# Gated linear attention and a soft mixture of experts: blocks of 128 tokens in place of two chunks of 64, y made transposed, odd head pairs reversed in time, and a combination in four row tiles

## The chip, the cores and the metric

The kernel runs on one core of a Trainium2 chip. The metric is the device time of one execution in microseconds (us). The engines of the core are named as in the profile: PE (matrix multiply; PEld is its weight load), DVE (VectorE), ACT (ScalarE), POOL (GpSimd) and SP (the queue that issues all the DMAs). Each engine works through its own queue in order, and waits where an operand isn't ready yet.

## The reference

First comes a linear attention with a decay, for 4 batches x 8 heads, 768 tokens, head size D = 48:

```
f = 1 / (1 + exp(-f_logit))
for t in range(S):
    state = f[:, :, t, :, None] * state + einsum('bhd,bhe->bhde', k[:, :, t], v[:, :, t])
    y[:, :, t] = einsum('bhd,bhde->bhe', q[:, :, t], state)
```

Its output, as x of 3072 tokens x 384, goes through a soft mixture with 32 slots, four for each of 8 experts:

```
logits = x @ phi                                   # 3072 x 32
d = softmax of logits over the tokens              # per slot
slot_input = d.T @ x                               # 32 x 384
slot_out[e] = relu(slot_input[e] @ w1[e]) @ w2[e]  # 384 -> 1024 -> 384, per expert
c = softmax of logits over the slots               # per token
out = c @ slot_out                                 # 3072 x 384
```

Everything is float32.

## The kernel before

**Attention.** Six blocks of 128 tokens for each of 4 batches make 24 blocks. A tile holds the 8 heads as 4 head pairs: the first head of a pair in partitions 0 to 47, the second in 64 to 111. The recurrence is turned into matmuls by the running sum of ln(1 + exp(-f_logit)) inside a chunk of C = 64 tokens, two chunks in a block; the second head of each pair is stored with its two chunks exchanged. exp and ln (L374, L377) are made for two blocks at once on ACT. Then, for each block: the scan L395 (DVE, 512 elements wide; `chain` is 0 where a new sum begins), the exponentials g and p (L398, L401, ACT), the decay of whole chunks `pend` (L405, L406, two copies on POOL), k times g and q times p (L409, L412, POOL). PE transposes k (L417), and L420 copies it to SBUF. L441 makes k^T v of both chunks (16 small matmuls), and DVE adds that to the state and multiplies by the decay, once for each chunk (L444 and L449, 192 wide). L460 multiplies q by the states (16 matmuls of 48 columns), L430 makes the scores k^T q (16 matmuls of 64 columns), L433 masks the later keys out of them (DVE, 512 wide), and L470 adds scores times v to the result of L460 (16 matmuls of 48 columns). L476 copies y to SBUF with tokens in the partitions (`xr`); L509 transposes it (3 transposes) and L512 copies that to `xT`.

**Mixture in the block phase.** Every four blocks a *unit* makes the logits (L527) with their maximum and exponential over tokens (L533, L536), transposes both (L539, L542), multiplies the exponential by x (L546, L549), and takes the softmax over the slots of its 512 tokens (L555 to L578, tiles `ce` and `cm`). The last two steps, L575 and L578, split the result into a high and a low part in the fp32r format (tile `c`), which L583 transposes and L586 copies to `cts`.

**Tail.** Maximum over all units, L643 (slot inputs), L682 (the product with w1, 48 matmuls of 512 columns), relu, transposes, L716 (the product with w2, in three parts of 128 output columns), and for each part L741: six matmuls of 128 x 512 in fp32r, copied out by L747 and stored by L751, 128 output columns x 512 tokens each.

**What sets the order.** All operations are given to a planner (`Plan`), which lays out every engine's queue ahead of time: of the operations that are ready it takes the one that can start first, and among those within 0.12 us of each other the one with the lowest due time, `T(n, stage) = 3.6 * n + stage` for block n. Durations come from formulas such as `t_dve`. PSUM is planned the same way: three two-bank tiles ("pair") for L441, L460 with L470, and L430, and two one-bank tiles ("one", `sg` in the profile) for the rest. Twelve 8 KB homes (`hm`) take w1; w2 goes into buffers of the block phase that have come free.

The scan, for example, is a single line over the whole block, and its place in DVE's queue is the planner's choice:

```
add(f"scan{n}", {"DVE": 0.06 + 0.0021 * 512}, scan, r=[L, "chain"], w=[CB], prio=T(n, 1))
add(f"g{n}", {"ACT": t_act(512)}, exp_g, r=[CB], w=[G], prio=T(n, 1.4))
```

Of the kernel before, what the change touches and what calls it, by code (L numbers as in the profile page):

```python
# [9 lines left out]
F32R = mybir.dt.float32r  # L10
# [6 lines left out]
C = 64  # L17
BT = 128
NB = S // BT
NN = B * NB  # L20
# [15 lines left out]
NX = 8  # L36
# [28 lines left out]
def t_dve(n, psum=False):  # L65
    return 0.09 + 0.00105 * n + (0.06 if psum else 0)


def t_pool(n):
    return 0.1 + 0.0023 * n  # L70


def t_pe(n):

    return 0.06 + 0.00086 * n


class Plan:
# [40 lines left out]
    def schedule(self):  # L119
# [13 lines left out]
        while ready:  # L133
            best = None
            for n in ready:
                op = ops[n]
                for e, us in op["eng"].items():
# [5 lines left out]
                    if op["kind"]:  # L143
                        if not pool[op["kind"]]:
                            continue
                        t = max(t, min(pool[op["kind"]])[0] + self.LAT)
# [14 lines left out]
            if op["kind"]:  # L161
                x = min(pool[op["kind"]])
                pool[op["kind"]].remove(x)
                self.bank[op["psum"]] = (op["kind"], x[1])
# [29 lines left out]
def gla_soft_moe_kernel(ctx: ExitStack, tc: tile.TileContext, q, k, f, v, fd, kd, vd, phi, w1, w2, out):  # L194
# [17 lines left out]

    pairs = [pp.tile([128, 2, 512], F32, tag=f"pr{i}", name=f"pr{i}") for i in range(3)]
    ones_ = [pp.tile([128, 512], F32, tag=f"sg{i}", name=f"sg{i}") for i in range(2)]
    plan = Plan({"pair": [0, 1, 2], "one": [0, 1]})

    def bank(handle):
        kind, x = plan.bank[handle]
        return (pairs if kind == "pair" else ones_)[x]


    AF_, AK, AQ, AV, AC, AP = (P([128, HOME], n) for n in ("af", "ak", "aq", "av", "ac", "ap"))
    homes = [P([128, HOME], f"hm{i}") for i in range(NHOME)]
    NK, NQ, NV, NC, NSS = 4, 4, 4, 3, 4

    def part(t, x, n, **kw):
        return t[:, x : x + n].rearrange("p (a t) -> p a t", **kw)

    fb = [AF_[:, 1024 * i : 1024 * i + 1024].rearrange("p (n a t) -> p n a t", n=2, a=PR) for i in range(2)]
# [3 lines left out]
    cb = [part(AC, 512 * i, 512, a=PR) for i in range(NC)]  # L233
    gb = [part(AV, 1536, 512, a=PR), part(AC, 1536, 512, a=PR)]
    kp = [part(AP, 512 * i, 512, a=H) for i in range(2)]
    sc = [AP[:, 1024 + 512 * i : 1536 + 512 * i].rearrange("p (r a t) -> p r a t", r=2, a=PR) for i in range(2)]
    st = [P([128, PR, D], f"st{i}") for i in range(NSS)]
    sa = [P([128, PR, D], f"sa{i}") for i in range(2)]
    xr = P([128, NX, DM], "xr")
    xT = P([128, 3, UB, 128], "xT")  # L240
    cts = P([128, NN, 128], "cts", F32R)
    c4 = P([128, UB, 4, NS], "c4", F32R)
    ce, cm = P([128, UB, NS], "ce"), P([128, UB], "cm")
    el = P([128, 2, 128], "el")
    lt, et = P([128, 128], "lt"), P([128, 128], "et")
    pin = P([128, NU, DM], "pin")

    nmx, sms = P([128, NU], "nmx"), P([128, NU], "sms")
    ident, ones, same = (P([128, 128], n) for n in ("ident", "ones", "same"))
    tri, chain = P([128, C], "tri"), P([128, 2 * PR, C], "chain")  # L250
    phs = P([128, 3, NS], "phs")
    pend = P([128, NN, 2, PR], "pend")
# [4 lines left out]
    s4, sob = P([128, DM], "s4", F32R), P([128, DM], "sob")  # L257
    hx = P([128, 512], "hx")
    gok, gbad = P([128, 4], "gok"), P([1, 1], "gbad", I32)
    hs = [flat(xT)[:, 512 * i : 512 * i + 512] for i in range(3)] + [hx]  # L260
    hT = flat(xr)[:, :2048].rearrange("p (j k m) -> p j k m", j=2, k=8)
    ARENA = {
        "af": (AF_, [("f", i) for i in range(2)] + [("f", i, x) for i in range(2) for x in range(2)]),
        "ak": (AK, [("k", i) for i in range(NK)]),
        "ac": (AC, [("c", i) for i in range(NC)] + [("g", 1)]),
        "ap": (AP, [("kp", i) for i in range(2)] + [("sc", i) for i in range(2)]),
        "aq": (AQ, [("q", i) for i in range(NQ)]),
        "av": (AV, [("v", i) for i in range(NV)] + [("g", 0)]),
# [15 lines left out]
    def c_tri(e):  # L284

        for c in range(2):
            cs = slice(C * c, C * c + C)
            nc.gpsimd.affine_select(tri[cs], ones[cs, :C], pattern=[[1, C]], compare_op=ALU.is_ge, fill=0.0, base=0, channel_multiplier=-1)

    def c_chain(e):  # L290

        nc.vector.memset(chain, 1.0)
        nc.vector.memset(chain[:, :, 0], 0.0)
# [4 lines left out]
    def c_kv(e):  # L298
        for t in pairs:
            nc.vector.memset(t, 0.0)  # L300
# [19 lines left out]
    add("chain", {"DVE": 0.4}, c_chain, w=["chain"])  # L320
    add("ident", {"POOL": 0.8}, c_ident, w=["ident"])
    add("tri", {"POOL": 0.5}, c_tri, r=["ones"], w=["tri"], prio=1)
    add("kv0", {"DVE": 2.4}, c_kv, w=["kv0"])
    add("same", {"DVE": 0.5}, c_same, r=["ident"], w=["same"], prio=20)
    add("emask", {"POOL": 1.0}, c_emask, w=["emask"], prio=30)
    for x in range(9):
        add("warm", {"PE": 0.3}, warm(x), r=["ones"], w=["warm"], prio=100)


    homes_ = [(t, [("home", i)]) for i, t in enumerate(homes)]  # L330
# [3 lines left out]
    w2at, at = {}, 0  # L334
    for p, j, kh in W2:
        w2at[p, j, kh] = at
        at += 16 * (CUT[p + 1] - CUT[p])

    def load_w1(x):
        t = w1p[W1[x]]  # L340
        return lambda e: nc.sync.dma_start(t, w1[x])

    def load_w2(p, j, kh):
        n = 16 * (CUT[p + 1] - CUT[p])
        t, at = w2p[p, j, kh], w2at[p, j, kh]
        return lambda e: nc.sync.dma_start(t[:, :n], w2[:, at : at + n])


    def T(n, stage):
        return 3.6 * n + stage  # L350
# [7 lines left out]
    def load_f(n, cnt):  # L358
        i, o = n // 2 % 2, n % 2
        load(fb[i][:, o : o + cnt], f[:, n : n + cnt], f"f{n}", [("f", i, x) for x in range(o, o + cnt)], T(n, -10), 262144 * cnt)  # L360

    def loads(n):
        load(kb[n % NK], k[:, n], f"k{n}", [("k", n % NK)], T(n, -8.5), 262144)
        load(qb[n % NQ], q[:, n], f"q{n}", [("q", n % NQ)], T(n, -8), 262144)
        load(vb[n % NV], v[:, n], f"v{n}", [("v", n % NV)], T(n, -7), 196608)

    def exp_f(n, cnt):

        i, o = n // 2, n % 2
        es = n if n < 2 else i + 1  # L370
        t = flat(fb[i % 2][:, o : o + cnt])
        ks = [("f", i % 2, x) for x in range(o, o + cnt)]
        add(
            f"exp{n}", {"ACT": t_act(512 * cnt) + 0.09}, lambda e: nc.scalar.activation(t, t, AF.Exp, scale=-1.0, accum_out=esum[:, es : es + 1]),  # L374
            w=[*ks, "esum"], prio=T(n, 0),
        )
        add(f"ln{n}", {"ACT": t_act(512 * cnt)}, lambda e: nc.scalar.activation(t, t, AF.Ln, bias=1.0), w=ks, prio=T(n, 0.5))  # L377

    def block(n):
        b, m = divmod(n, NB)  # L380
        l_ = fb[n // 2 % 2][:, n % 2]
        c_, g_, k_, q_, v_, kp_, sc_ = cb[n % NC], gb[n % 2], kb[n % NK], qb[n % NQ], vb[n % NV], kp[n % 2], sc[n % 2]
        L, CB, G, K, Q, V, KP, SC = ("f", n // 2 % 2, n % 2), ("c", n % NC), ("g", n % 2), ("k", n % NK), ("q", n % NQ), ("v", n % NV), ("kp", n % 2), ("sc", n % 2)
        X = ("x", n % NX)
        x_ = xr[:, n % NX]

        S = [("st", (2 * n + j) % NSS) for j in range(3)]
        s_ = [st[(2 * n + j) % NSS] for j in range(3)]
        steps = [j for j in range(2) if (m, j) != (NB - 1, 1)]
        begun = [j for j in range(2) if (m, j) != (0, 0)]  # L390
# [3 lines left out]
        def scan(e):  # L394
            nc.vector.tensor_tensor_scan(flat(c_), flat(chain), flat(l_), 0.0, op0=ALU.mult, op1=ALU.add)  # L395

        def exp_g(e):
            nc.scalar.activation(flat(g_), flat(c_), AF.Exp)  # L398

        def exp_p(e):  # L400
# [572 lines left out]
```

## Time and profile before

| | before |
|---|---|
| median of 3 runs | 220.26 us (218.66 to 224.37) |
| the profiled execution | 220.23 us, of which the profile's span is 218.5 us |
| mean granted PE clock | 0.84 |
| PE busy | 163.8 us (75%) |
| DVE busy | 129.3 us (59%) |
| ACT busy | 103.1 us (47%) |
| POOL busy | 82.6 us (38%) |
| moved by DMA | 54.22 MB |

Busy time counts an engine's instructions; a matmul in float32 leaves two records. The span falls into a start (until the first transposes of k, at 9.95 us), the block phase (until the last y is in SBUF, at 156.26 us), and the tail. In a timeline the columns are start, duration, engine, line, operation, output <- inputs, number of instructions, and in brackets the engine's idle time before it with what ended it.

### The profile page before, as it was taken

How to read it: one execution, taken by the hardware profiler on the slowest of the kernel's cores; microseconds unless marked ns; L12 is line 12 of the kernel's file. 1: busy time of each engine (PE TensorE's matmuls, PEld its weight loads, DVE VectorE, ACT ScalarE, POOL GpSimd, SP SyncE). 2: the span in 40 equal slices, each digit the busy share in tenths (PEclk: the TensorE clock that was granted, in tenths of full speed). 3: DMA queues.
4: the chain of work that ended last, by engine and by line, in shares of the span. 5: the costliest groups of instructions: out<-in, count | busy, mean ns of one | idle time of the engine just before them, and what ended most of it. 6: DMA issues, size and time to landing. Idle time of an engine off the chain costs nothing.

```text
span 218.5 us, 9188 instructions
## 1 busy us (share of the span) xinstructions
PE 163.8 (75%) x4046; PEld 119.8 (55%) x4046; DVE 129.3 (59%) x257; ACT 103.1 (47%) x198; POOL 82.6 (38%) x116
## 2 busy tenths in 40 slices
PE   7487879839586786994498866888764999699840
PEld 7476767628464575764386655756523234565510
DVE  7677785797979592369669999987360023010120
ACT  4466655382654645528567774734330112025540
POOL 3145875470777404505994834980000000000000
PEclk9967665896999796559589999999955699999975
DMA  6999998688798498959546644545694499507491
GB/s 188 343 392 404 390 297 283 214 256 307 228 348 306 140 357 281 393 156 329 174 143 186 165 157 142 157 171 195 202 387 187 139 351 418 250 6 288 185 359 51
DMA packets 17874, 54.22 MB, mean 248 GB/s; under 512 B 2336, under 2 KB 5408, under 8 KB 14752
## 3 DMA queue, kind: packets, MB, share of 16 engines
q1 hardware_dynamic: 17824, 53.53, 69.5%
q8 instruction: 34, 0.56, 1.0%
q14 instruction: 16, 0.13, 0.2%
HBM read 48.81 MB, written 4.72 MB: 245 GB/s over the span
## 4 chain that ended last, share of the span: by engine, by line
PE 37%; DVE 16%; issue 13%; ACT 10%; POOL 5%; DVEq 0%; POOLq 0%; ACTq 0%
PE sg L682 6%; PE sg L716 5%; DVE st L449 4%; PE pr L460 3%; PE sg L417 3%; POOL ak L409 3%; DVE ac L395 3%; PE pr L470 3%; PE sg L741 3%; PE pr L430 3%; ACT hm L747 2%; PE sg L509 2%; DVE ap L433 2%; PE pr L441 2%; PE sg L527 2%
## 5 line engine op out<-in xcount | busy, mean ns | idle before, releaser
L412 POOL TENSOR_TENSOR aq<-aq,ac 128x512 f32<-128x512 f32 x23 | 31.4, 1364 | 2.5 <-issue 1.9
L395 DVE TENSOR_TENSOR_SCAN ac<-chain,af 128x512 f32<-128x512 f32 x24 | 30.3, 1268 | 1.7 <-POOL pend L406 1.5
L409 POOL TENSOR_TENSOR ak<-ak,av 128x512 f32<-128x512 f32 x11 | 15.2, 1383 | 40.0 <-issue 27.3
L470 PE MATMUL pr<-av,ap 64*64 64x48 f32 x768 | 19.4, 244 | 11.1 <-DVE ap L433 9.2
L417 PE MATMUL sg<-ident,ak 128*128 128x128 f32 x96 | 19.3, 338 | 8.4 <-POOL ak L409 5.7
L470 PEld LDWEIGHTS pr<-av,ap 64*64 64x64 f32 x768 | 16.2, 155 | 15.9 <-DVE ap L433 12.3
L449 DVE TENSOR_TENSOR st<-sa,pend 128x192 f32<-128x192 f32 x35 | 23.3, 665 | 2.1
L460 PE MATMUL pr<-st,aq 48*64 48x48 f32 x704 | 22.2, 247 | 2.8 <-DVE st L449 2.1
L430 PE MATMUL pr<-aq,ak 48*64 48x64 f32 x768 | 20.3, 243 | 4.1 <-issue 4.1
L460 PEld LDWEIGHTS pr<-st,aq 48*64 48x64 f32 x704 | 18.4, 158 | 7.3 <-DVE st L449 3.0
L430 PEld LDWEIGHTS pr<-aq,ak 48*64 48x64 f32 x768 | 17.1, 154 | 5.6 <-issue 5.6
L433 DVE TENSOR_TENSOR ap<-pr,tri 128x512 f32<-128x512 f32 x24 | 16.3, 680 | 5.6 <-PE pr L430 5.5
L417 PEld LDWEIGHTS sg<-ident,ak 128*128 128x128 f32 x96 | 13.1, 170 | 11.5 <-POOL ak L409 6.7
L409 POOL TENSOR_TENSOR ak<-ak,ac 128x512 f32<-128x512 f32 x11 | 15.0, 1368 | 10.2 <-issue 7.4
L420 ACT COPY ap<-sg 128x512 f32<-128x512 f32 x21 | 12.3, 584 | 13.5 <-PE sg L417 13.2
L441 PE MATMUL pr<-av,ap 64*48 64x48 f32 x704 | 15.8, 233 | 2.6 <-ACT ap L420 1.7
L444 DVE TENSOR_TENSOR sa<-pr,st 128x192 f32<-128x192 f32 x40 | 14.1, 352 | 6.1 <-ACT xr L476 1.9
L441 PEld LDWEIGHTS pr<-av,ap 64*48 64x48 f32 x704 | 13.2, 145 | 5.5 <-ACT ap L420 2.4
L509 PE MATMUL sg<-ident,xr 128*128 128x128 f32 x72 | 14.8, 322 | 1.3 <-ACT xr L476 1.3
L401 ACT ACTIVATE ac<-ac 128x512 f32<-128x512 f32 x24 | 15.2, 631 | 0.6
L374 ACT ACTIVATE af<-af 128x1024 f32<-128x1024 f32 (+1 forms) x13 | 12.9, 992 | 4.4 <-DMA af<-in_f_dram 4.4
L476 ACT COPY xr<-pr 128x384 f32<-128x384 f32 x17 | 8.1, 477 | 14.3 <-PE pr L470 14.2
(125 smaller groups left out, 257.6 us busy)
## 6 DMA issues: line engine op xcount, KB each, us to landing
hm<-in_w_dram SPq DMA_DIRECT2D x18, 1024.0 KB, 7.6
ak<-in_k_dram SPq DMA_DIRECT2D x24, 256.0 KB, 4.1
aq<-in_q_dram SPq DMA_DIRECT2D x24, 256.0 KB, 4.3
af<-in_f_dram SPq DMA_DIRECT2D x11, 512.0 KB, 6.0
av<-in_v_dram SPq DMA_DIRECT2D x24, 192.0 KB, 4.7
out_dram<-hm SPq DMA_DIRECT2D x6, 512.0 KB, 2.8
out_dram<-hm SPq DMA_DIRECT2D x6, 256.0 KB, 3.0
af<-in_w_dram SPq DMA_DIRECT2D x1, 1024.0 KB, 4.7
```

The source lines that it names most:

```text
L395: nc.vector.tensor_tensor_scan(flat(c_), flat(chain), flat(l_), 0.0, op0=ALU.mult, op1=ALU.add)
L401: nc.scalar.activation(flat(c_), flat(c_), AF.Exp, scale=-1.0)
L409: tt(e)(flat(k_), flat(k_), flat(g_), op=ALU.mult)
L412: tt(e)(flat(q_), flat(q_), flat(c_), op=ALU.mult)
L417: nc.tensor.transpose(pk[:, a], k_[:, a], ident)
L430: nc.tensor.matmul(ps[half[c], r, a], k_[rows[r], a, half[c]], q_[rows[r], a, half[c]], start=True, stop=True)
L433: tt(e)(sc_, sc_at(), tri.unsqueeze(1).unsqueeze(1).broadcast_to([128, 2, PR, C]), op=ALU.mult)
L441: nc.tensor.matmul(pk[C * r : C * r + D, j, a], kp_[half[c], h, :D], v_[half[c], h], start=True, stop=True)
L449: tt(e)(s_[j + 1], src, pend[:, n, j].unsqueeze(2).broadcast_to([128, PR, D]), op=ALU.mult)
L460: nc.tensor.matmul(py[half[j], r, a], q_[rows[r], a, half[j ^ r]], s_[j][rows[r], a], start=a == 0, stop=False, skip_group_check=True)
L470: nc.tensor.matmul(py[half[j], r, a], sc_[half[c], r, a], v_[half[c], 2 * a + r], start=j not in begun and a == 0, stop=a == PR - 1, skip_ ...
L509: nc.tensor.transpose(px[:, c], x_[:, 128 * c : 128 * c + 128], ident)
```

## The change

**Blocks of 128.** The chunk is now the block: one sum over 128 tokens, one state step for each block. Odd head pairs are stored reversed in time (k, q, f and v), and their scans L381 and L382 run apart: one forward over the two even pairs, one backward over the two odd ones. The exponentials (L396, L397) and the copies of `pend` are made for two blocks at once. L451 (k^T v) has 8 matmuls with 128 rows, into a one-bank tile; there is one L454 and one L458 for each block.

**y transposed.** L468 and L477 have the states and v as stationary operand, and q and the scores as moving one: 8 matmuls of 128 columns each. The result has head dimensions in the partitions, so L480 copies it straight to `xT`, and what is transposed (L510, 4 transposes) is the `xr` that L546 needs. The logits (L527) have 4 padded row groups instead of 3 (16 matmuls).

**No scores of later keys.** In L439 a key of the second half meets 64 queries only, a key of the first half 128; the scores have a two-bank tile of their own, and the mask L442 is 1024 wide for a block.

**Slot softmax.** It keeps the logits in `ltok`, is made for two units at once (256 wide), without a split in two parts, and its due time lies behind the block phase: `T(NN, 12)`.

**Combination.** For each of three parts there are four groups of two float32 matmuls of 32 rows x 384 columns, each in its own row tile; L735 copies 768 columns, and 384 KB are stored for each group.

**Loads.** q, k, v and f are contiguous for each block in DRAM; w1 and w2 come as four runs of 2 KB for each partition in place of one of 8 KB. Two more PSUM tiles are cleared at the start, and the warming matmuls wait for that. The planner has other duration formulas for DVE and POOL, and a pace of 3.8 in place of 3.6 in `T`.

```diff
-    plan = Plan({"pair": [0, 1, 2], "one": [0, 1]})
+    plan = Plan({"sc": [0], "pair": [1, 2], "one": [0, 1]})
...
     def T(n, stage):
-        return 3.6 * n + stage
+        return 3.8 * n + stage
...
+        def scan(x):
+            def fn(e):
+                cx, lx = flat(cb[i % 2][:, x]), flat(fb[i % 2][:, x])
+                nc.vector.tensor_tensor_scan(cx[:, : 2 * BT], chain, lx[:, : 2 * BT], 0.0, op0=ALU.mult, op1=ALU.add)
+                nc.vector.tensor_tensor_scan(cx[:, 2 * BT :][:, ::-1], chain, lx[:, 2 * BT :], 0.0, op0=ALU.mult, op1=ALU.add)
+            return fn
...
+        for x in xs:
+            add(f"scan{n + x - o}", {"DVE": 2 * t_scan(256)}, scan(x), r=[ks[x - o], "chain"], w=[cs[x - o]], prio=T(n + x - o, -1))
+        add(f"g{n}", {"ACT": t_act(w)}, lambda e: nc.scalar.activation(flat(g_), flat(c_), AF.Exp), r=cs, w=gs, prio=T(n, 1))
...
         def scores(e):
-            ps = sc_at()
+            ps = bank(("sc", n)).rearrange("p r (a t) -> p r a t", a=PR)
             for a in range(PR):
                 for c in range(2):
+                    at = half[c ^ (a % 2)]
                     for r in range(2):
-                        nc.tensor.matmul(ps[half[c], r, a], k_[rows[r], a, half[c]], q_[rows[r], a, half[c]], start=True, stop=True)
+                        nc.tensor.matmul(ps[at, r, a, HT * c :], k_[rows[r], col(a), at], queries(r, a)[:, HT * c :], start=True, stop=True)
...
         def kv(e):
-            pk = bank(("kv", n))[:, :, : PR * D].rearrange("p j (a e) -> p j a e", a=PR)
+            pk = bank(("kv", n))[:, : PR * D].rearrange("p (a e) -> p a e", a=PR)
             for a in range(PR):
-                for j in steps:
-                    for r in range(2):
-                        h, c = 2 * a + r, j ^ r
-                        nc.tensor.matmul(pk[C * r : C * r + D, j, a], kp_[half[c], h, :D], v_[half[c], h], start=True, stop=True)
...
+                for r in range(2):
+                    nc.tensor.matmul(pk[rows[r], col(a)], kp_[:, col(a), rows[r]], v_[:, 2 * a + r], start=True, stop=True)
...
         def inter(e):
             py = y_at()
             for a in range(PR):
-                for j in begun:
-                    for r in range(2):
-                        nc.tensor.matmul(py[half[j], r, a], q_[rows[r], a, half[j ^ r]], s_[j][rows[r], a], start=a == 0, stop=False, skip_group_check=True)
+                for r in range(2):
+                    at = 64 * (r ^ (a % 2))
+                    nc.tensor.matmul(py[at : at + D, r, a // 2], s0[rows[r], col(a)], queries(r, a), start=a < 2, stop=False, skip_group_check=True)
...
         def intra(e):
             py = y_at()
             for a in range(PR):
-                for c in range(2):
-                    for r in range(2):
...
+                for r in range(2):
+                    at = 64 * (r ^ (a % 2))
+                    nc.tensor.matmul(py[at : at + D, r, a // 2], v_[:, 2 * a + r], sc_[:, r, a], start=first and a < 2, stop=a >= 2, skip_group_check=True)
...
+    def slots(th):
+        x = slice(2 * UB * th, 2 * UB * th + 2 * UB)
...
+        sp = T(NN, 12) + th
...
         def combine(p, x):
...
+            def fn(e):
+                for y in range(2):
+                    gs = slice(64 * (x % 2) + 32 * y, 64 * (x % 2) + 32 * y + 32)
+                    nc.tensor.matmul(
+                        bank(("cb", p, x))[:, y, :384], s4[gs, CUT[p] : CUT[p + 1]], cts[gs, 3 * (x // 2) : 3 * (x // 2) + 3], start=True, stop=True,
+                    )
+            return fn
```

Two places show what the planner makes of this. On DVE, before, in the middle of the block phase: the slot softmax of unit 2 (L564 to L578), the two state steps of block 13, and then the scan of block 14:

```order
L564 TENSOR_REDUCE cm<-ce 128x4
L565 TENSOR_SCALAR cm<-cm 128x4
L566 RECIPROCAL cm<-cm 128x4
L569 TENSOR_TENSOR ce<-ce,cm 128x128
L575 CAST c_94<-ce 128x8x32
L476 COPY xr<-pr_62 128x2x4x48
L578 TENSOR_TENSOR c_94<-ce,c_94 128x8x32
L444 TENSOR_TENSOR sa_89<-pr_63,st_87 128x192
L449 TENSOR_TENSOR st_88<-sa_89,pend 128x192
L444 TENSOR_TENSOR sa_90<-pr_63,st_88 128x192
L449 TENSOR_TENSOR st_85<-sa_90,pend 128x192
L395 SCALAR_TENSOR_TENSOR ac<-chain,af 128x512
```

After, on DVE near the same scan: the state step and the mask of block 10, then both scans of block 14 (those of block 15 and the mask of block 11 follow):

```order
L454 TENSOR_TENSOR sa<-sg_66,st_89 128x192
L458 TENSOR_TENSOR st_90<-sa,pend 128x192
L442 TENSOR_TENSOR as<-pr_62,tri 128x1024
L381 SCALAR_TENSOR_TENSOR ac<-chain,af 128x256
L382 SCALAR_TENSOR_TENSOR ac<-chain,af 128x256
```

The scan of block 14 has moved from behind the mask of block 12 to a place ahead of the mask of block 11, and no slot softmax stands ahead of it there. The slot softmax of units 0 to 3 still stands on DVE among the masks of later blocks, that of units 4 and 5 behind the last one.

On PE, before, at blocks 6 to 9: scores of block 7, transposes of x of block 6, of k of block 8, L470 of block 7, L441 of block 8, and transposes of k of block 9 and of x of block 7:

```order
L430 MATMUL pr_62<-aq,ak 64x64 x16
L509 MATMUL sg_66<-ident,xr 128x128 x3
L417 MATMUL sg_65<-ident,ak 128x128 x4
L470 MATMUL pr_64<-av,ap 64x48 x16
L441 MATMUL pr_63<-av,ap 48x48 x16
L417 MATMUL sg_66<-ident,ak 128x128 x4
L509 MATMUL sg_65<-ident,xr 128x128 x3
```

After, on PE, at the same blocks: transposes of k of block 8 and of y of block 6, L477 of block 7, L451 of block 8, L468 of block 8 and the transposes of y of block 7:

```order
L428 MATMUL sg_65<-ident,ak 128x128 x4
L510 MATMUL sg_66<-ident,xT 128x128 x4
L477 MATMUL pr_63<-as,av 48x128 x8
L451 MATMUL sg_65<-av,kp_86 48x48 x8
L468 MATMUL pr_64<-aq,st_90 48x128 x8
L510 MATMUL sg_66<-ident,xT 128x128 x4
```

A block has fewer and wider matmuls, and L451 now takes its turn with the transposes in the two `sg` tiles. Along PE's queue in the block phase the shape of the tile (128 rows by 128 columns, 64 by 64, 128 by 64 and so on) changes 136 times, against 104 before.

503 lines of the change are left out of this document (232 added, 271 removed).

## The prediction

> **What bounds the kernel now.** I read the page first, then the busy time of each stage, then the timeline where engines wait.
>
> ```profile
> span 218.5 us, 9188 instructions
> PE 163.8 (75%) x4046; PEld 119.8 (55%) x4046; DVE 129.3 (59%) x257; ACT 103.1 (47%) x198; POOL 82.6 (38%) x116
> PEclk9967665896999796559589999999955699999975
> PE 37%; DVE 16%; issue 13%; ACT 10%; POOL 5%; DVEq 0%; POOLq 0%; ACTq 0%
> ```
>
> No engine is full. The chain that ended last is spread over PE, DVE and ACT, as where short steps hand over to each other; PE leads it. The clock row is uneven in the first half and flat at 9 in most of the second. The timeline gives the stages:
>
> ```profile
> 9.95 0.63 PE L417 MATMUL sg<-ident,ak 128*128 128x128 f32 x4 [2.51 <-issue]
> ...
> 155.78 0.48 ACT L476 COPY xr<-pr 128x384 f32<-128x384 f32 x1 [0.55 <-PE pr L470]
> ...
> 168.76 0.26 PE L643 MATMUL sg<-wd,pin 128*32 128x32 f32 x1 [3.24 <-issue]
> 169.47 5.21 PE L682 MATMUL sg<-hm,si 128*32 128x512 f32 x32
> ...
> 185.09 1.08 PE L716 MATMUL sg<-af,xr 128*32 128x128 f32 x32
> ...
> 210.99 0.58 ACT L747 COPY hm<-sg 128x512 f32<-128x512 f32 x1
> ```
>
> The start takes 9.95 us; the blocks run until 156.26 (155.78 + 0.48), 146.3 us or 6.10 for each of 24; then 13.2 us to the first product with w1, 15.6 to the first with w2, 26.5 until the last copy (211.57), and 6.9 for the last store. Two thirds of the time lie in the blocks, so the windows there decide, first over all engines, then for the masks L433 alone, which count the blocks:
>
> ```profile
> core 0: us, PE busy (x) PEld busy (x) DVE busy (x) ACT busy (x) POOL busy (x), PEclk, DMA share, GB/s
> 10.00:30.00 20.00, 15.62 (x438) 12.90 (x438) 15.46 (x26) 13.37 (x23) 13.01 (x16) 0.73 1.02 382
> 10.00:110.00 100.00, 75.69 (x2012) 60.32 (x2016) 71.78 (x130) 56.22 (x107) 54.33 (x65) 0.77 0.84 291
> 110.00:158.00 48.00, 38.23 (x1326) 30.30 (x1319) 39.93 (x82) 27.98 (x55) 25.96 (x34) 0.99 0.53 168
> 10.00:158.00 148.00, 113.92 (x3326) 90.62 (x3327) 111.71 (x212) 84.20 (x161) 80.29 (x98) 0.84 0.74 251
> ```
>
> ```profile
> 10.00:110.00 100.00, 9.53 (x14) 0.77 0.84 291
> 110.00:158.00 48.00, 6.79 (x10) 0.99 0.53 168
> ```
>
> There are two speeds. From 10 to 110 us 14 blocks pass, 7.1 us each, at a clock of 0.77; from 110 to 158 ten, 4.8 each, at 0.99. At full clock a block costs PE 3.82 us (38.23 / 10) and DVE 3.99: both are over 80% full there, and a faster kernel must make both shorter or keep the clock up. Why the first stretch is slower shows in its stalls:
>
> ```profile
> 49.05 0.65 PE L583 MATMUL sg<-ident,c 128*128 128x128 f32 x4 [3.34 <-DVE c L578]
> ...
> 98.76 1.22 DVE L395 TENSOR_TENSOR_SCAN ac<-chain,af 128x512 f32<-128x512 f32 x1
> ...
> 100.07 0.63 ACT L398 ACTIVATE av<-ac 128x512 f32<-128x512 f32 x1
> ...
> 100.83 1.92 POOL L409 TENSOR_TENSOR ak<-ak,av 128x512 f32<-128x512 f32 x1 [10.23 <-issue]
> ```
>
> PE stands 3.34 us because the transpose of the slot softmax is next in its queue and DVE hasn't finished L578; everything behind it stands too. POOL idles 10.23 us: its product waits for L398, that for block 14's scan, and the scan (98.76) was queued on DVE behind unit 2's slot softmax and block 13's state steps.
>
> **PE's work for a block.** I cost it by warm rows:
>
> ```profile
> 146.29 0.58 PE L441 MATMUL pr<-av,ap 64*48 64x48 f32 x32
> ...
> 147.18 0.68 PE L470 MATMUL pr<-av,ap 64*64 64x48 f32 x32 [0.32 <-DVE ap L433]
> 147.80 0.66 PE L417 MATMUL sg<-ident,ak 128*128 128x128 f32 x4
> ...
> 149.46 0.49 PE L509 MATMUL sg<-ident,xr 128*128 128x128 f32 x3
> 149.88 0.68 PE L460 MATMUL pr<-st,aq 48*64 48x48 f32 x32
> 150.39 0.66 PE L430 MATMUL pr<-aq,ak 48*64 48x64 f32 x32
> ...
> 185.99 1.06 PE L716 MATMUL sg<-ak,xr 128*32 128x128 f32 x32
> ```
>
> Before: 0.66 + 0.58 + 0.68 + 0.66 + 0.68 + 0.49 = 3.75. L716 is the row for 128 columns: from 185.09 to 185.99, 32 records take 0.90 us, 28 ns each, with four column tiles side by side (so 112 ns for one alone), and its 1.08 leaves a tail of 0.18. After:
> - transposes of k 0.66, of y 0.66 (four now);
> - k^T v, half as many matmuls of twice the rows: 0.50, between 0.29 (half of L441) and 0.58;
> - L468, 16 records in four quadrants: 16 x 0.028 + 0.18 = 0.63, up to 1.08 if only two run side by side;
> - scores, columns 1.5 times: (0.66 - 0.18) x 1.5 + 0.18 = 0.90;
> - L477, 128 rows, so two column tiles at most: 16 x 0.056 + 0.18 = 1.08. Its bounds are 0.63 (as four tiles) and 1.97 (16 x 0.112 + 0.18, no overlap). I take the middle, since L716 shows that column tiles do overlap.
>
> That is 4.43, so 0.68 more: fewer instructions, but more columns. The measured 3.82 becomes 4.50; units give about 0.07 back: three of the four transposes of 49.05 (0.65) go, 0.49 in four blocks or 0.12 for each, and a fourth row group of logits takes some of that (so 0 to 0.12).
>
> Tile shapes change 32 times more. L460 begins at 149.88 and lasts 0.68, yet L430, with the same shape, begins 0.17 before its end; L509 to L460, across a change, overlaps 0.07. So a change costs about 0.10 us, 3.2 in all, 0.13 for a block: 4.56. [...]
>
> **DVE's work for a block.**
>
> ```profile
> 10.00:158.00 148.00, 24.70 (x39) 2.53 (x5) 0.84 0.74 251
> ...
> L444 DVE TENSOR_TENSOR sa<-pr,st 128x192 f32<-128x192 f32 x40 | 14.1, 352 | 6.1 <-ACT xr L476 1.9
> L433 DVE TENSOR_TENSOR ap<-pr,tri 128x512 f32<-128x512 f32 x24 | 16.3, 680 | 5.6 <-PE pr L430 5.5
> L395 DVE TENSOR_TENSOR_SCAN ac<-chain,af 128x512 f32<-128x512 f32 x24 | 30.3, 1268 | 1.7 <-POOL pend L406 1.5
> ...
> 10.00:158.00 148.00, 11.13 (x25) 1.55 (x5) 0.00 (x0) 0.84 0.74 251
> ```
>
> The first row is L449 on DVE and POOL: 0.633 us each on DVE. The new order has 20 on DVE in place of 39, so 12.0 us go (19 x 0.633), and 16 of L444 in place of 40, 8.5. The last row is the slot softmax's tile `ce`: 11.1 go, but two thirds of the new one are still queued among the blocks; at half the old width for the split that is gone I put back 4. The mask grows by 512 columns at the pace between L444 and L433, (680 - 352) / 320 = 1.03 ns: 0.525 x 24 = 12.6 more. Two half scans for one add an instruction each, 1.2 by the small fixed costs (bounds 0 and 24 x 0.35 = 8.4, a whole L444). 111.7 - 12.0 - 8.5 - 11.1 + 4 + 12.6 + 1.2 = 97.9, 4.1 for a block. ACT (84.2) and POOL (80.3, less half the copies of `pend`) stay below.
>
> **The pace.** PE is now the fullest. In the second stretch the busiest engine was 83% full; the stalls above go with the scan's earlier place, so I take 87%: 4.56 / 0.87 = 5.25 us. I assume the clock of the second stretch throughout, as PE would stand less. DMA doesn't bind: all w1 loads come ahead of block 17's, and the first 100 us moved 29.1 MB, which at the 382 GB/s of the first window take 76 us, 4.5 for each of 17 blocks. That w1 comes in 2 KB runs I put at nothing; the cover is this slack of 0.7 us a block. Those waits gone, L477's wait for the longer mask is late next.
>
> **The ends.**
>
> ```profile
> 7.88 0.63 ACT L374 ACTIVATE af<-af 128x512 f32<-128x512 f32 x1 [2.89 <-DMA af<-in_f_dram]
> ...
> 8.51 0.61 ACT L398 ACTIVATE av<-ac 128x512 f32<-128x512 f32 x1
> ...
> 9.15 0.69 DVE L409 TENSOR_TENSOR ak<-ak,av 128x512 f32<-128x512 f32 x1 [1.96 <-ACT av L398]
> ...
> L409 POOL TENSOR_TENSOR ak<-ak,av 128x512 f32<-128x512 f32 x11 | 15.2, 1383 | 40.0 <-issue 27.3
> L741 PE MATMUL sg<-cts,s 128*128 128x512 f32 x18 | 8.8, 510 | 1.9 <-ACT hm L747 0.8 <-DVE s L737 0.7
> L747 ACT COPY hm<-sg 128x512 f32<-128x512 f32 x16 | 9.3, 586 | 9.1 <-PE sg L741 8.9
> ```
>
> Start: g of block 0 is now queued on ACT behind ln of block 1 too (0.63 more), and the first product of k is on POOL (1.38 in place of 0.69): 9.95 + 1.3 = 11.2. Behind the last y the transpose and its copy leave the path to the logits (about 1.1), and I let half of L643's 3.24 stall go: 10.5 (9 to 13). The product with w1 stays 15.6. Combination: six matmuls for a part become eight, in row tiles that overlap in pairs. A record of 384 columns alone takes 0.34 (112 ns x 3), a pair of matmuls has four: 0.34 if all four row tiles work side by side, 0.67 in twos, 1.34 one after another. I take 0.67, which is hidden behind 768-wide copies of about 0.88 (586 x 1.5) on two engines; at 1.34 it would show, 12 x 0.46 = 5.5. With L737's wait gone (three times about 0.3) and 12 copies of 0.88 for 18 of 0.59 on two engines, 26.5 becomes 24 (to 30). Last store 6.9.
>
> **Sum:** 11.2 + 24 x 5.25 + 10.5 + 15.6 + 24 + 6.9 = 194.2 of span, 68.2 of it outside the blocks. The profiled execution took 220.23 for 218.5, 1.7 more, and stands at the median of 220.26: forecast **196 us**, 186 to 206 by itself.
>
> **Rivals.**
> - *Filled.* L477 at its low bound makes PE 4.11, level with DVE. With both 92% full, which no stretch shows, a block takes 4.45: 106.8 + 68.2 + 1.7 = 176.7.
> - *The clock stays low.* Against my assumption: from 10 to 30 us PE was 78% busy, fuller than later, at 0.73. If the first 14 blocks stay at 0.77, PE needs 4.56 / 0.77 / 0.87 = 6.8 each: 95.3 + 52.5 + 68.2 + 1.7 = 217.7, no change. [...]
> - *Slower.* Place: L477. If its column tiles don't overlap, each block costs PE 0.9 more (5.46), and with a low clock too it takes 8.15 us for 14 blocks and 6.28 for ten: 114.1 + 62.8 + 68.2 + 1.7 = 246.8. It decides from a mean pace of (218.5 - 68.2) / 24 = 6.26 on. Against it stands L716's overlap; for it that no row shows 128 rows with 64-column tiles.
> - *The slot softmax doesn't move.* Units 0 to 3 stay among the blocks, and two stalls like that of 3.34 would give 196 + 6.7 = 203, inside the forecast's own range.
>
> **How the numbers follow.** Forecast with the softmax's stalls 0.50, filled 0.14, low clock 0.18, slower 0.18. About 2% (4.4 us) is what a measurement of this kernel tells from no change. The low clock's 217.7 lies near that bound (215.9), so a third of it counts as faster: 0.50 + 0.14 + 0.06 = 0.70 faster, 0.12 the same, 0.18 slower. The range goes from 174 to 220: it holds all but the slower case and a little at the low end.
>
> **What will show it.** Right: clock 0.95 or more from 10 to 110 us, masks 5 to 5.5 us apart in both stretches, a warm L477 of about 1.1, masks of 1.2, DVE near 98 in the blocks, no POOL gap of 10 us. Wrong: a clock near 0.77 in the first half (then the forecast falls even with its sums right), L477 near 2.0, or an engine other than PE fullest.

## The result, and the profile after

The changed kernel takes 186.28 us (median of four runs, 184.69 to 190.37) against 219.69 us for the kernel before beside it; the ratio is 0.847, with a 95% interval of 0.836 to 0.857. The forecast was 196 us. Some executions take a few per cent longer at a lower clock (here 190.37 us at 0.931, beside 184.69 to 187.12 at 0.959 to 0.975); a ratio with an interval leaves them out, a median doesn't. In the profiled execution (185.45 us, span 183.7) the page begins:

```profile
span 183.7 us, 6935 instructions
PE 151.2 (82%) x2974; PEld 109.7 (60%) x2974; DVE 123.0 (67%) x203; ACT 97.4 (53%) x169; POOL 72.2 (39%) x91
PEclk9999998799999999999999999999999999999985
PE 54%; DVE 18%; issue 6%; ACT 6%; DMA 5%; POOL 5%; SPq 0%; POOLq 0%; DVEq 0%; ACTq 0%
```

The clock row tells most: it holds 9 nearly throughout, where before it went up and down between 5 and 9 for half the span. PE's part of the chain that ended last has grown from 37% to 54%. The timeline gives the stages:

```profile
10.54 0.66 PE L428 MATMUL sg<-ident,ak 128*128 128x128 f32 x4 [1.35 <-POOL ak L420]
...
132.56 0.58 ACT L480 COPY xT<-pr 128x512 f32<-128x512 f32 x1 [1.28 <-PE pr L477]
...
138.81 1.43 PE L633 MATMUL sg<-wd,pin 128*32 128x32 f32 x144 [0.97 <-DVE wd L624]
...
140.59 3.64 PE L672 MATMUL sg<-hm,si 128*32 128x512 f32 x32
...
154.63 1.08 PE L706 MATMUL sg<-af,xr 128*32 128x128 f32 x32
...
175.79 0.80 ACT L735 COPY hm<-pr 128x768 f32<-128x768 f32 x1 [0.31 <-PE pr L729]
```

| stage | before | forecast | after |
|---|---|---|---|
| until the first transposes of k | 9.95 | 11.2 | 10.54 |
| the 24 blocks | 146.3 (6.10 each) | 126 (5.25) | 122.6 (5.11) |
| last y to the products with w1 | 13.2 | 10.5 | 7.45 |
| products with w1 | 15.6 | 15.6 | 14.0 |
| products with w2, combination | 26.5 | 24 | 22.0 |
| last store | 6.9 | 6.9 | 7.1 |

So 23.7 of the 34.8 us come from the blocks. The windows there, over all engines, and then those of the mask L442, which count the blocks:

```profile
core 0: us, PE busy (x) PEld busy (x) DVE busy (x) ACT busy (x) POOL busy (x), PEclk, DMA share, GB/s
10.00:70.00 60.00, 51.24 (x1052) 39.44 (x1052) 51.20 (x73) 42.07 (x69) 34.52 (x38) 0.97 1.04 378
70.00:130.00 60.00, 53.37 (x1132) 41.29 (x1124) 49.77 (x79) 36.54 (x68) 34.03 (x36) 1.00 0.73 242
10.00:130.00 120.00, 104.62 (x2174) 80.73 (x2174) 100.97 (x151) 78.61 (x136) 68.55 (x73) 0.99 0.88 310
```

```profile
10.00:30.00 20.00, 3.96 (x4) 1.00 1.05 386
30.00:50.00 20.00, 4.53 (x4) 0.91 1.05 382
...
110.00:130.00 20.00, 4.89 (x4) 1.00 0.64 217
```

The two speeds of the kernel before (7.1 and 4.8 us a block) are gone: four masks pass in every 20 us, with full DMA queues and without. At full clock the changed kernel is no faster: 5.0 us a block against 4.8. The kernel before kept that pace even inside its slow part where the clock was full for longer: from 53.20 to 73.70 us the granted clock is 1.00, and four masks pass in 20.5 us. **All the gain of the blocks lies in the stretch where the clock used to be low**, and the question for the runs is what keeps it up.

### The profile page after: what moved, and what is told of

It reads as the page before. It is cut to its first block, busy times and chain, and to the rows that moved or that the text cites. A ratio compares the mean times of both kernels' runs of the same rounds, so it can differ in the third digit from the quotient of the medians.

```text
span 183.7 us, 6935 instructions
## 1 busy us (share of the span) xinstructions
PE 151.2 (82%) x2974; PEld 109.7 (60%) x2974; DVE 123.0 (67%) x203; ACT 97.4 (53%) x169; POOL 72.2 (39%) x91
## 4 chain that ended last, share of the span: by engine, by line
PE 54%; DVE 18%; issue 6%; ACT 6%; DMA 5%; POOL 5%; SPq 0%; POOLq 0%; DVEq 0%; ACTq 0%
PE pr L477 8%; PE pr L439 7%; PE sg L706 6%; PE sg L672 6%; DMA ak<-in_k_dram 5%; PE sg L428 5%; DVE as L442 5%; DVE ac L382 4%; POOL ak L420 4%; DVE ac L381 4%; PE pr L729 4%; PE sg L510 4%; PE pr L468 3%; PE sg L547 3%; PE sg L451 3%
## 5 line engine op out<-in xcount | busy, mean ns | idle before, releaser
L420 POOL TENSOR_TENSOR ak<-ak,ag 128x512 f32<-128x512 f32 x23 | 31.0, 1350 | 45.1 <-ACT ag L396 28.9
L442 DVE TENSOR_TENSOR as<-pr,tri 128x1024 f32<-128x1024 f32 x24 | 29.2, 1218 | 8.8 <-PE pr L439 8.7
L477 PE MATMUL pr<-as,av 128*48 128x128 f32 x384 | 26.7, 283 | 7.1 <-DVE as L442 7.0
L477 PEld LDWEIGHTS pr<-as,av 128*48 128x48 f32 x384 | 20.5, 125 | 12.4 <-DVE as L442 9.4
L381 DVE TENSOR_TENSOR_SCAN ac<-chain,af 128x256 f32<-128x256 f32 x24 | 21.5, 895 | 0.4 <-ACT af L393 0.4
L439 PE MATMUL pr<-aq,ak 48*64 48x64 f32 (+1 forms) x768 | 21.6, 250 | 0.0
L382 DVE TENSOR_TENSOR_SCAN ac<-chain,af 128x256 f32<-128x256 f32 x24 | 21.0, 877 | 0.0
L439 PEld LDWEIGHTS pr<-aq,ak 48*64 48x64 f32 x768 | 17.9, 133 | 3.5 <-issue 2.9
L510 PE MATMUL sg<-ident,xT 128*128 128x128 f32 x96 | 15.4, 283 | 2.1 <-DVE xT L480 1.2
L390 ACT ACTIVATE af<-af 128x1024 f32<-128x1024 f32 (+1 forms) x13 | 12.9, 996 | 6.7 <-DMA af<-in_f_dram 6.7
L468 PE MATMUL pr<-aq,st 48*48 48x128 f32 x320 | 13.3, 283 | 3.1 <-issue 1.8
L396 ACT ACTIVATE ag<-ac 128x1024 f32<-128x1024 f32 (+1 forms) x13 | 12.9, 991 | 5.0 <-DVE ac L382 5.0
L735 ACT COPY hm<-pr 128x768 f32<-128x768 f32 x9 | 6.9, 801 | 15.8 <-PE pr L729 15.8
L480 ACT COPY xT<-pr 128x512 f32<-128x512 f32 x16 | 9.4, 585 | 9.0 <-PE pr L477 8.8
L510 PEld LDWEIGHTS sg<-ident,xT 128*128 128x128 f32 x96 | 10.4, 140 | 5.4 <-ACT xT L480 1.3
L397 ACT ACTIVATE ac<-ac 128x1024 f32<-128x1024 f32 (+1 forms) x13 | 12.9, 992 | 0.4
L393 ACT ACTIVATE af<-af 128x1024 f32<-128x1024 f32 (+1 forms) x13 | 12.9, 993 | 0.2
```

Source lines behind the costliest of these rows:

```text
L381: nc.vector.tensor_tensor_scan(cx[:, : 2 * BT], chain, lx[:, : 2 * BT], 0.0, op0=ALU.mult, op1=ALU.add)
L382: nc.vector.tensor_tensor_scan(cx[:, 2 * BT :][:, ::-1], chain, lx[:, 2 * BT :], 0.0, op0=ALU.mult, op1=ALU.add)
L390: f"exp{n}", {"ACT": t_act(w) + 0.09}, lambda e: nc.scalar.activation(flat(l_), flat(l_), AF.Exp, scale=-1.0, accum_out=esum[:, es : es + 1]),
L393: add(f"ln{n}", {"ACT": t_act(w)}, lambda e: nc.scalar.activation(flat(l_), flat(l_), AF.Ln, bias=1.0), w=ks, prio=T(n, -2.5))
L420: tt(e)(flat(k_), flat(k_), flat(g_), op=ALU.mult)
L439: nc.tensor.matmul(ps[at, r, a, HT * c :], k_[rows[r], col(a), at], queries(r, a)[:, HT * c :], start=True, stop=True)
```

## The experiments

Two theories stood at first. By the prediction's, the *stall theory*, PE waited in the first stretch for late scans and for the slot softmax, and its clock dropped for that. The rival, the *DMA theory*, blames the w1 loads, which run in just that stretch. A third came out of these runs: the *density theory*, by which it also counts how much of the PE array the work fills. Times are compared with the kernel before on the same chip; its median was 222.63 us beside the first four runs, 226.5 beside the next four and 223.43 beside the last four.

**The kernel before without w1 traffic.**

```diff
-        return lambda e: nc.sync.dma_start(t, w1[x])
+        n = HOME if x == 0 else 16
+        return lambda e: nc.sync.dma_start(t[:, :n], w1[x][:, :n])
```

> The kernel before, with 11 of the 12 w1 loads cut to 16 columns for each partition (all products with w1 read the first w1 tile, so the output is another); the order of every queue in the block phase is unchanged. Stall theory (the first 14 blocks take 7.1 us each because PE waits for late scans and the slot softmax, and its clock drops for that): the order is the same, so the time stays, 215 to 221 us, clock below 0.87. DMA theory (the w1 loads delay q, k, v and f in the first 100 us): the first 14 blocks run at the 4.8 us of the later ones, 14 x 2.3 = 32 us less, 185 to 195 us.

Measured: 218.71 us, ratio 0.983 (0.976 to 0.990). The window of the profiled execution (221.10 us), in the columns of the windows above:

```profile
10.00:110.00 100.00, 78.86 (x2024) 63.61 (x2028) 71.75 (x129) 56.29 (x106) 53.20 (x64) 0.70 0.56 177
```

Queues that were 84% busy are 56% busy, and in those 100 us there are still 14 masks, at a clock of 0.70. A gain of 1 to 2.4% is far from the 185 to 195 us of the DMA theory, which falls.

**The kernel before with the slot softmax behind the blocks.**

```diff
-        sp = t0 + (2 if not late else 8)
+        sp = T(NN, 12) + u      # made after the last block, from a tile of its own for each unit
```

> The kernel before, with the slot softmax (L555 to L586) of all six units behind the last block, nothing else. Stall theory: the 3.3 us waits for L578 go and DVE loses 11 us in the blocks, clock above 0.88, 203 to 213 us (most of the softmax is hidden behind the products with w1). DMA theory: no change in the first 14 blocks, 217 to 223 us.

Measured: 218.63 us against 222.63 (the lowest are 214.37 and 218.50). That is far short of the expected 203 to 213.

**The kernel before with earlier scans.**

```diff
-        add(f"scan{n}", ..., prio=T(n, 1))
+        add(f"scan{n}", ..., prio=T(n, -1))
```

> The kernel before, with the due times of the load of f, of exp and ln, and of the scan put earlier to those of the changed kernel (-12, -3, -2.5 and -1 in place of -10, 0, 0.5 and 1), nothing else. Stall theory: POOL's waits of up to 10 us for a scan go, clock above 0.88, 203 to 213 us. DMA theory: loads come no sooner, 217 to 223 us.

Measured: 214.73 us, ratio 0.979 (0.948 to 1.011), clocks of 0.84 and 0.82: some gain at most, and in neither of the two ranges.

**Both together.**

> The kernel before with both edits, slot softmax behind the blocks and earlier scans. Stall theory: nearly all of the first stretch's excess goes, about 5.2 us for each block, 188 to 202 us, clock above 0.93; the wider blocks of the changed kernel then gain little by themselves. DMA theory: 215 to 223 us. Theory that the wider blocks (fewer instructions) make the gain: 212 to 222 us.

Measured: 214.95 us (212.64 and 217.27) against 222.63. The windows:

```profile
10.00:110.00 100.00, 81.20 (x2220) 65.01 (x2223) 73.05 (x114) 57.90 (x108) 59.39 (x67) 0.75 0.82 287
110.00:158.00 48.00, 38.92 (x1112) 29.24 (x1106) 35.75 (x77) 23.24 (x51) 22.11 (x26) 0.89 0.63 220
52.90:63.10 10.20, 10.20 (x274) 8.77 (x270) 4.80 (x9) 4.30 (x9) 1.44 (x2) 0.50 0.75 243
```

The edit does what it should: PE no longer waits for the softmax, and it is 81% busy in place of 76%. But only 16 masks pass in 100 us in place of 14, the clock is 0.75, and the time lies in the range of the third expectation, that the wider blocks make the gain. Other waits remain (PE stands up to 3.1 us for a mask), so this run doesn't rule out idle time by itself. The last row does more: the clock fell at 49.5 us, around two waits of 1.23 and 1.34 us, and then stayed at half through 10.2 us in which PE never paused. In the changed kernel a wait of 1.81 us, from 72.62 us on, left the clock full. So the stall theory isn't the whole story: without the two stalls that it named, the narrow blocks stay slow. What they show instead can already be seen in the kernel before, in two windows of 10 us:

```profile
30.00:40.00 10.00, 9.59 (x216) 8.29 (x214) 5.69 (x9) 3.77 (x6) 5.06 (x8) 0.52 0.75 254
120.00:130.00 10.00, 7.03 (x220) 5.23 (x219) 9.39 (x18) 7.22 (x16) 5.82 (x8) 1.00 0.57 177
```

PE is 96% busy at a clock of 0.52, and 70% busy at 1.00, with as many instructions (216 and 220). A busy PE wasn't enough for the clock here; at 0.52 it was simply busy for longer with about as many records.

**Useless dense work in the kernel before.** That gave the density theory, which the next two runs put to the test with equal numbers of matmuls of equal length.

```diff
         def turn_k(e):
             pk = bank(("kt", n)).rearrange("p (a t) -> p a t", a=PR)
+            nc.tensor.matmul(pk[:, 0], ident, ident, start=True, stop=True)
...     # the same in tr
```

> The kernel before with one useless float32 matmul of a full 128 x 128 tile with 128 columns (ident by ident, about 0.22 us warm) ahead of the transposes L417 and of L509, in the PSUM tile that those overwrite: 48 in all, about 0.45 us of PE for each block. Density theory (the clock is granted by how much of the PE array works, and small tiles of 48 to 64 columns work too little of it): the clock rises to 0.90 or more and the time falls in spite of the added work, 198 to 214 us. Idle theory (the clock depends only on how long PE has no instruction): the clock stays below 0.87 and the added 10.8 us show, 222 to 234 us.

Measured: 220.79 us (217.64 and 223.94) against 226.5, with clocks of 0.86 and 0.85 where the kernel before had 0.78 to 0.81 beside it. It isn't the 0.90 that was expected, and the time lies between the two ranges. In other runs the kernel before reached 0.85 too, so this rise alone proves little; the next run is what it has to be compared with.

**Useless thin work in the same places.**

```diff
+            nc.tensor.matmul(pk[:32, 0], ident[:32, :32], ident[:32], start=True, stop=True)
```

> The control to that: the same number of useless matmuls in the same places, with the same 128 columns, but in a 32 x 32 tile, a sixteenth of the array. Density theory: clock as before (0.80 to 0.87), time 222 to 234 us. Idle theory: the same as with the full tile, whatever that is.

Measured: 239.04 us, ratio 1.054 (1.039 to 1.069). The window:

```profile
10.00:110.00 100.00, 91.45 (x1868) 65.70 (x1869) 60.96 (x117) 47.38 (x90) 42.07 (x55) 0.60 0.76 261
```

PE is 91% busy, the most of all runs with narrow blocks, and its clock is the lowest, 0.60. The clock of the whole execution, 0.71 and 0.73, and the time also lie beyond the range of the density theory, which had thin work leave the clock as it was. The full tile and the thin one differ by 18 us and 0.12 or more of clock, with the same number of matmuls, whose shortest records take nearly the same time (275 ns with the full tile, 267 with the thin one). That the two differ is what density predicts and idle time doesn't: with the thin tiles PE waits least and has the lowest clock. One thing isn't separated: the thin tile has another shape than the transposes behind it, so each adds a change of shape, which the full tile doesn't.

**Stalls put into the changed kernel.**

```diff
         def mask(e):
-            tt(e)(
+            for _ in range(4 if n in (4, 8, 12, 16) else 1):
+              tt(e)(
```

> The changed kernel, with the mask L442 made four times over in blocks 4, 8, 12 and 16 (same result), so that DVE, and PE behind it, stands 3.7 us longer there, 14.6 us in all. Idle theory: the clock drops after each of these stalls as in the kernel before and the blocks after it are slow too, over 205 us, clock below 0.92. Density theory: the wide matmuls win the clock back at once, 190 to 201 us, clock 0.94 or more.

Measured: 208.65 us, ratio 0.920 (0.909 to 0.931), clock 0.90. That is what the idle theory expected, and more than the 190 to 201 us of the density theory. Windows of 5 us around the second of the stalls that PE feels:

```profile
60.00:65.00 5.00, 2.76 (x78) 1.91 (x70) 4.71 (x7) 3.87 (x9) 1.33 (x2) 1.00 0.96 331
65.00:70.00 5.00, 3.28 (x25) 1.73 (x25) 3.56 (x6) 0.00 (x0) 4.06 (x5) 0.66 0.32 108
70.00:75.00 5.00, 4.72 (x96) 3.65 (x92) 3.42 (x6) 4.47 (x8) 0.00 (x0) 1.00 0.98 361
```

The clock does fall after a long wait (PE stands for 3.96 of the 10 us from 60.00 to 70.00), to 0.66, and is full again in the next window; after two other stalls it stayed at half for 6.8 us, after this one for 3.4. The added masks are 12 x 1.22 = 14.6 us; the span is 23.2 longer (206.9 against 183.7), so each stall costs about 2 us beyond itself. So both theories hold in part: behind long waits the clock fell in either kernel (in the kernel before to 0.50 from 49.80 to 53.20 us, behind L583's wait of 3.34 us), and the two differ in how soon it returns: in these wide blocks within 3.4 to 6.8 us, while in the narrow ones it stood at 0.52 through 10 us of a PE that was 96% busy.

**The changed kernel with scores made twice.**

```diff
-                    for r in range(2):
+                    for r in (0, 1, 0, 1):
```

> The changed kernel with the scores L439 made twice over (same result), 0.72 us more on PE for each block at full clock. If PE sets the pace of the blocks, as the prediction has it: 24 x 0.72 = 17 us more, 199 to 206 us. If DVE or DMA set it: under 192 us.

Measured: 198.89 us, ratio 0.877 (0.866 to 0.888), clock 0.977; the span is 13.7 us longer. So 13.7 of the 17.3 us of added PE work show, four fifths: PE mostly sets the pace.

**The changed kernel with all of the slot softmax behind the blocks.**

```diff
-        add(f"smx{th}", ..., w=[CM], prio=sp)
+        add(f"smx{th}", ..., w=[CM], prio=sp, after=[...])      # the last block's put_y
```

> The changed kernel with the slot softmax of units 0 to 3 too held back behind the last block (those of units 4 and 5 are there already), nothing else. If the softmax among the blocks costs what DVE spends on it there (about 4 us) or a stall of PE with a drop of the clock: 180 to 184 us. If it is hidden, as PE sets the pace: 184 to 188 us. If it now delays the combination: over 188 us.

Measured: 190.12 us, ratio 0.863 (0.847 to 0.879). This interval overlaps that of the changed kernel (0.836 to 0.857), so no loss is shown, and no sign of the gain of 2 to 6 us: among the wide blocks the softmax is hidden.

**The changed kernel without w1 traffic.**

> The changed kernel with 11 of the 12 w1 loads cut to 16 columns for each partition (all products with w1 read the first w1 tile, so the output is another). The DMA queues of the changed kernel are full from 10 to 80 us. If the loads set the pace there: 4.6 us for each block in place of 5.0 in that stretch, 176 to 181 us. If PE sets it, as the prediction has it: 184 to 188 us.

Measured: 192.11 us (189.87 and 194.35) against 223.43, above both ranges. The stretch from 10 to 70 us is the one to look at:

```profile
10.00:70.00 60.00, 51.70 (x1055) 39.65 (x1056) 51.30 (x73) 41.96 (x68) 35.16 (x38) 0.97 0.69 226
```

In this execution (194.35 us) the queues are 69% busy there in place of 104%, and yet every engine has done the same number of instructions, within 4, as with all of the traffic. Full DMA queues don't set the pace here. What this execution loses it loses later, where its clock is lower (0.91 from 70 to 130 us, against 1.00); why is not shown.

**Thin useless work in the changed kernel.**

```diff
+            nc.tensor.matmul(pk[:32, 0], ident[:32, :32], ident[:32], start=True, stop=True)
...     # ahead of L428, and the same ahead of L510
```

> The changed kernel with one useless matmul of 128 columns in a 32 x 32 tile ahead of each block's transposes L428 and L510, as in the control on the kernel before: 0.45 us of PE for each block, 10.8 us in all. If the wide matmuls of the changed kernel hold the clock with room to spare: clock above 0.94, 192 to 199 us. If its clock is near the edge and thin work tips it over, as it did before: clock below 0.90, over 203 us.

Measured: 193.07 us (191.53 and 194.61) against 223.43, clock 0.98, as the first expectation had it. The same 48 thin matmuls that cost the narrow blocks 12.5 us and 0.08 of the clock cost the wide ones about 6 us of span (189.8 against 183.7) and no clock. They bring changes of shape here too, and the changed kernel has more of those than the kernel before to begin with (136 against 104), so it isn't these by themselves that slowed the narrow blocks.

**Earlier scans, late softmax and dense work together in the kernel before.**

> The kernel before with the slot softmax behind the blocks, the earlier scans and the full-tile useless matmuls together. If low clock comes of long waits and of thin work together: clock 0.90 or more, 200 to 212 us. If the narrow blocks can't hold the clock by any of these: clock below 0.87, 213 to 225 us.

Measured: 212.07 us, ratio 0.966 (0.946 to 0.985). The windows:

```profile
10.00:110.00 100.00, 82.69 (x2229) 67.84 (x2231) 69.93 (x111) 55.97 (x105) 58.94 (x68) 0.83 0.80 281
110.00:158.00 48.00, 40.65 (x1201) 31.81 (x1193) 36.49 (x77) 25.03 (x54) 22.18 (x26) 0.97 0.65 224
```

Of all runs with narrow blocks this has the highest clock, 0.89, with 10.8 us of useless work on board. It ends at the edge of the first expectation, 212 us and 0.90. In the clock the remedies add up; in time they don't: the lowest run, 211.31 us, is hardly below the 212.64 of the two remedies without the dense work, and far from the wide blocks.

## Why the prediction was right, and where its reasons were not

**PE's sum held.** Warm rows of the changed kernel, for one block's worth of PE work:

```profile
123.83 0.66 PE L428 MATMUL sg<-ident,ak 128*128 128x128 f32 x4
...
125.33 0.53 PE L451 MATMUL sg<-av,kp 128*48 128x48 f32 x16
125.78 0.90 PE L439 MATMUL pr<-aq,ak 48*64 48x128 f32 x32
...
126.62 0.66 PE L510 MATMUL sg<-ident,xT 128*128 128x128 f32 x4
...
127.20 0.65 PE L468 MATMUL pr<-aq,st 48*48 48x128 f32 x16
...
128.16 1.08 PE L477 MATMUL pr<-as,av 128*48 128x128 f32 x16
```

They make 4.48 where 4.43 was worked out, term by term within 0.03; L477 takes the 1.08 of two column tiles side by side, so the slower rival, which had them not overlap, is out. By the window from 70 to 130 us, twelve masks, a block costs PE 4.45 (53.37 / 12) against the forecast's 4.56.

**The pace held, 5.11 against 5.25**, and with it the assumption of a full clock (0.99 from 10 to 130 us). The rival of a low clock is out, and so is the filled one: PE is 87% full, the share that was assumed, not 92%.

**The reason for the clock was wrong.** The step that failed is this one: the stalls go with the scan's earlier place, and the clock of the second stretch then holds "as PE would stand less". Taking those stalls out of the kernel before left its clock at 0.75 from 10 to 110 us (0.77 before) and gained about 3%. The clock does fall after waits (to 0.66 in the windows of the made stalls), but the wide blocks won it back within 3.4 to 6.8 us, while those of the kernel before took up to 13.65, and without the two stalls half clock still lasted 10.2 and more. That the full clock came as assumed was, by the reason given for it, in part luck. The row that the prediction itself quoted against its assumption, 78% busy at 0.73, was the better guide to the cause. A busy PE alone didn't lift the clock either: 91% busy with thin tiles, it stood at 0.60.

**What the clock goes by** can be read further from the traces. Their own record of the clock has two values in the blocks, full and half, and keeps each for a multiple of 3.41 us. The half-clock stretches in the blocks of the kernel before last 3.41, 6.83, 10.24 or 13.65 us, those of the wide blocks in all their runs 3.41 or 6.83, and those of the narrow blocks with thin tiles added up to 54.61.

So all fourteen traces were divided, from 9 to 150 us, into pieces of 3.41 us, on whose borders all changes of the clock lie. The work that PE begins in a piece was weighed by how much of the array it fills: for each matmul record, its columns times the rows and columns of its tile as a share of 128 x 128, called full-tile columns here. In 108 pieces at half clock PE was at least 95% busy. The clock was full in the next piece after

- 5 of the 35 with fewer than 1300 full-tile columns,
- 9 of the 22 with 1300 to 1400,
- 47 of the 51 with more.

One bound of 1344 tells, whatever the busy time, what the next piece will be for 382 of the 397 pieces at full clock and 146 of the 165 at half clock, missing 6 of 241 in wide blocks and 28 of 321 in narrow ones. The best bounds on busy time, one for each case, tell it for 380 and 123. By this count a wait and narrow work come to the same: in the kernel before, the pieces from 46.39 us (PE 22% busy) and from 12.25 us (97% busy) begin 620 and 1196 full-tile columns, both below the bound, and half clock follows both.

An estimate from this suggests why narrow blocks then stay slow. Full-tile records of 128 columns begin 0.11 us apart in L510 at full clock, and 0.21 us apart in L417 of the kernel before at half (four from 32.22 us on take 1.06, the last 0.42 of them), so a piece holds about 4000 full-tile columns at full clock and 2000 at half. The bound is a third of the one, but two thirds of the other: at half clock even a PE that never waits would miss it with tiles that fill less than two thirds of the array. All this was found in the traces afterwards, and no run was made to test the bound.

The blocks of the kernel before spent 47.8 us at half clock, those of the changed kernel 3.4. With records 0.21 us apart at half clock in place of 0.11, I estimate that at most about half of the former, 24 us, was lost to the clock itself, beside the 23.7 gained; how much of the gain is the clock's and how much comes of shorter waits isn't separated.

**DVE's sum was nearly right through errors that partly cancel.** It came to 97.9; 102.66 were measured from 10 us to the last y at 133.14. The mask was sized well (1218 ns, worked out as 1.205 us). The half scans were not: I put 1.2 us for 24 blocks, by fixed costs that no run shows, and the groups show

```profile
L381 DVE TENSOR_TENSOR_SCAN ac<-chain,af 128x256 f32<-128x256 f32 x24 | 21.5, 895 | 0.4 <-ACT af L393 0.4
L382 DVE TENSOR_TENSOR_SCAN ac<-chain,af 128x256 f32<-128x256 f32 x24 | 21.0, 877 | 0.0
```

895 + 877 - 1268 = 504 ns, or 12.1 us, above even the upper bound of 8.4. The term that the sum lacked is the longer time of scans beside POOL's products (last section; 1.19 us on average for a half scan): half scans that none of them overlaps take 0.67 us, two of them 0.13 more than such a whole scan before (1.21), which makes 3.1 us in 24 blocks. Part of the error was made up for elsewhere: the slot softmax (tiles `ce` and `cm`) fell from 15.0 to 5.3 us on DVE, where I had taken off 7.1, and the second state step by 13.1, where I had 12.0. None of it mattered much, since PE sets the pace. With the softmax moved out altogether no gain showed, and no wait of PE in the blocks of the changed kernel is longer than 1.9 us, so the two stalls of 3.3 us that one rival had for it didn't come.

**The ends were forecast too long by 7.1 us**, two thirds of the whole difference of 10.5 in span. From the last y to the products with w1 it is 7.45 in place of 10.5: L633's stall of 3.24 went whole, not by half, and the matmuls ahead of it no longer run at half clock (0.55 from 158.00 to 169.00 us before, 1.00 from 133.00 to 140.50 now; L547 takes 0.85 us, L546 took 1.51). The first 32 records of the products with w1 took 5.21 before, at a clock of 0.69, and take 3.64 now, at 1.00; I had left that stage unchanged. The last stage but one took 22.0 in place of 24: the pairs of L729 need about 0.52 (12 records, three pairs, in 1.56), below the 0.67 that was taken with no row to show it, and the copies 0.80 and 0.96, not 0.88.

## What to carry to other kernels

Before costing a change by the work of each engine, look at the granted clock by stage: the blocks of this kernel spent 47.8 us at half clock, and busy time showed that as a full engine (96% busy at 0.52). Fewer, wider matmuls were worth it here at no saving in time at full clock (5.0 us a block against 4.8), with 3.4 us at half clock left; that narrow ones fill too little of the array to win the clock back after a wait is a reading of the traces that no run tested. And a stall that is seen next to a low clock is a suspect, not the cause: take it out of the old kernel and see whether the clock moves (here from 0.77 to 0.75).

## What was not expected of the hardware

A DVE scan took longer beside a POOL product: 1.81 us in place of 0.68 for a half scan. Two scans L381 of the changed kernel and the products on POOL around them:

```profile
41.30 1.81 DVE L381 TENSOR_TENSOR_SCAN ac<-chain,af 128x256 f32<-128x256 f32 x1
...
44.99 0.68 DVE L381 TENSOR_TENSOR_SCAN ac<-chain,af 128x256 f32<-128x256 f32 x1
```

```profile
41.29 1.27 POOL L423 TENSOR_TENSOR aq<-aq,ac 128x512 f32<-128x512 f32 x1
47.63 2.63 POOL L420 TENSOR_TENSOR ak<-ak,ag 128x512 f32<-128x512 f32 x2 [5.07 <-ACT ag L396]
```

The first scan begins with a POOL product and takes 1.81 us; the second, with POOL idle, 0.68. The whole trace of the changed kernel bears this out: the 28 half scans that no POOL product overlaps take 0.66 to 0.69 us each, the other 20 take 1.19 on average. It isn't only scans: L458, where it reads and writes SBUF alone, takes 0.36 us without such an overlap and up to 1.47 with one, while the mask L442, which reads PSUM, keeps to 1.19 to 1.23 either way. In the kernel before, 17 of the 24 scans had no POOL product beside them and took 1.21 on average, and the mean of all was 1.27. So the scans now run beside POOL's products more often, and that makes up most of their 504 ns a block. No run took POOL's products away to show what that would gain.
